# Interleaving independent matmul work into the transform stages of a one-core forward-and-backward kernel, with the TensorE order fixed by hand

## The chip, the cores and the metric

The kernel runs on one core of one Trainium2 chip. The metric is the device time of one execution in microseconds (us). Before the change the median was 1783.06 us in 5 runs (1782.24 to 1788.13).

Engines are named as the profile names them: PE is TensorE with its matmuls, PEld the weight loads of TensorE, DVE is VectorE, ACT is ScalarE, POOL is GpSimd, SP is SyncE. PSUM is the memory that the matmuls of this kernel write to; *evicting* a result means copying it out of PSUM.

## The reference, cut to what matters

The reference is a transformer-like block and its whole backward pass. S is 2048 rows, D is 576 columns, F is 4608 hidden columns, all in bfloat16.

```python
def _A_ref(x, w_r, w_i):                    # spectral filter
    X = rfft2(x.astype(float32)) * (w_r + 1j * w_i)
    return irfft2(X, s=(S, D)).astype(bfloat16)

def _B_ref(x, w_gate, w_up, w_down):        # gated bilinear unit
    return ((x @ w_gate) * (x @ w_up)) @ w_down

def _fwd_reference(x, ..., c, w_mod):
    sa, ca, ga, sb, cb, gb = split6(silu(c) @ w_mod)
    h = layernorm(x) * (1 + ca) + sa
    x = x + ga * _A_ref(h, w_r, w_i)
    h = layernorm(x) * (1 + cb) + sb
    return x + gb * _B_ref(h, w_gate, w_up, w_down)

def reference(..., grad_out):
    out, vjp = jax.vjp(_fwd_reference, ...)   # A_x, A_w_r, A_w_i, B_w_gate, B_w_up, B_w_down, c, w_mod
    return (out, *vjp(grad_out))              # nine outputs
```

## The kernel before

The FFTs are done as matmuls with table matrices. The kernel has three parts.

- **Head.** The six modulation vectors come from blocks of `w_mod`. Then come the layernorm, the forward transform in 8 *fold* steps and 8 *pair* steps, and the inverse transform over 16 row tiles, which yields `h2T`, the input of the gated unit. Beside this runs work that needs none of it: `ghhT = w_down @ (grad_out * gb)^T`. It consists of 72 *ghh units* of 10 matmuls of 512 columns each.
- **Main loop.** 18 iterations over pairs of F-blocks do gate, up, their gradients and the weight gradients.
- **Tail.** This has the layernorm backward with folds, the backward pairs, the backward inverse with the second layernorm backward, the `w_mod` gradients (*finish blocks*) and the down-projection of the forward output (the `po` matmuls).

The framework has a scheduler that chooses each engine's order. `manual_schedule` switches it off for an engine, whose order is then that of the program. Before the change only the main loop had it.

The parts that the change touches, with cuts:

```python
def d_inverse(j, wk, T, ut, fps, ev):          # inverse transform of one row tile
    pv = fps.tile([128, 2, 512], FP32, name="pv", tag="fa")
    ...                                        # 6 matmuls into pv
    vt = wk.tile([128, 2, FQ], BF, name="vt", tag="vt", bufs=3)
    evac(vt[:], pv[:, :, 0:FQ], ev)
    py = fps.tile([128, 2, 512], FP32, name="py", tag="fa")
    ...                                        # 4 matmuls on vt into py
    return py[:, :, 0:288]

with ExitStack() as hs:                        # head
    fps = pool(hs, "fps", bufs=2, space=PSUM)
    gps = pool(hs, "gps", bufs=2, space=PSUM)
    ...
    for hf in range(2):
        t8 = slice(8 * hf, 8 * hf + 8)
        nc.gpsimd.dma_start(gon[:, t8, 0:D], go_v[:, t8, :])
        nc.vector.tensor_tensor(out=gon[:, t8, 0:D], in0=gon[:, t8, 0:D], in1=bc(mods[:, MGB, :], 8), op=MUL)
        nc.vector.tensor_copy(gon[:, t8, D:DP], gon[:, t8, 512:D])
        nc.sync.dma_start_transpose(out=goT[:, t8, :, :]..., in_=gon[:, t8, :]...)
    ...
    for t0 in range(0, NT, 2):
        ...                                    # layernorm, modulation
        fold(wk, h, t0, hT, T, fps, "a" if (t0 // 2) % 2 == 0 else "v")
    for i in range(8):
        ...
        X = pair_fwd(i, wk, gt, T, hT, fps, "aaaa")
        Y = cmul(wk, X, load_wp(wk, i), False)
        pair_inv(i, Y, gbt, ut, fps, "va")
    for t0 in range(0, NT, 2):
        for j in range(2):
            py = d_inverse(t0 + j, wk, T, ut, fps, "a")
            nc.scalar.copy(halves(yg[:, j, :]), py)
        ...                                    # residual, second layernorm -> h2p
        if t0 % 8 == 6:
            nc.sync.dma_start_transpose(out=h2T[:, t8, :, :]..., in_=h2p[:, t8, :]...)

    for fb in range(NFB):                      # 36 blocks, 2 ghh units each
        ...
        for k in range(2):
            pg = gps.tile([128, 2, 512], FP32, name="ghp", tag="gh")
            for b in range(2):
                ts_ = slice(8 * k + 4 * b, 8 * k + 4 * b + 4)
                for m in range(5):
                    r = slice(0, 128) if m < 4 else slice(64, 128)
                    nc.tensor.matmul(pg[:, b, :], lhsT=wdT[r, m, :], rhs=goT[r, ts_, m, :], start=(m == 0), stop=(m == 4))
            nc.scalar.copy(st[:, 8 * k:8 * k + 8, :], pg[:]...)

with ExitStack() as bs:                        # main loop
    ...
    bs.enter_context(tc.manual_schedule(engines={ET.PE}))
    ...

with ExitStack() as ts:                        # tail: the same step functions, then
    ...
    def finish_block(b, q):
        ...
        nc.vector.reciprocal(out=rc[:], in_=(opcb if b in (MSB, MCB) else opca))
    ...
    wdr = [slot(2, [128, 18, D], "wdr0"), up.tile([128, 18, D], BF, name="wdr1")]
    ...                                        # loads of w_down
    for tp_i in range(NT // 2):                # down-projection, 8 pairs of row tiles
        ...                                    # loads of hl, x1, grad_out
        for j in range(2):
            po = ops.tile([128, 2, 512], FP32, name="po")
            for fb in range(NFB):
                for h in range(2):
                    nc.tensor.matmul(po[:, h, 0:288], lhsT=hl[:, fb, j * 128:(j + 1) * 128], rhs=wdr[fb // 18][...], ...)
```

Of the kernel before, what the change touches and what calls it, by code (L numbers as in the profile page):

```python
# [8 lines left out]

FP32 = mybir.dt.float32  # L10
BF = mybir.dt.bfloat16
# [86 lines left out]
def build(ctx, tc, A_x, A_w_r, A_w_i, B_w_gate, B_w_up, B_w_down, c_in, w_mod, grad_out,  # L98
# [23 lines left out]
    gx1_d = dram("gx1_d", [128, NT, D], BF)  # L122
    ghhT_d = dram("ghhT_d", [F, S], BF)
# [11 lines left out]
    nc.vector.memset(ones_bf[:], 1.0)  # L135
    ones_f = glob.tile([128, 128], FP32, name="ones_f")
    nc.vector.memset(ones_f[:], 1.0)
    mods = glob.tile([128, 6, D], BF, name="mods")
# [42 lines left out]
    def fold(wk, h, t0, hT, T, fps, eng):  # L181
# [4 lines left out]
        nc.vector.tensor_tensor(out=eo[:, :, 545:576], in0=h[:, :, 257:288], in1=h[:, :, 319:288:-1], op=SUB)  # L186
        r2 = slice(t0 * 8, t0 * 8 + 16)
# [10 lines left out]
    def pair_fwd(i, wk, gt, T, hT, fps, ev):  # L198
        k2a, k2b = PAIRS[i]
        zt = wk.tile([128, 2, 2, FQ], BF, name="zt", tag="w")  # L200
        for kk, kap in enumerate((k2a, k2b)):
            pz = fps.tile([128, 2, 512], FP32, name="pz", tag="fa")
            for c in range(2):
                for mi in range(3):
                    m = (2 * c, 2 * c + 1, 4)[mi]
                    nc.tensor.matmul(pz[:, c, 0:FQ], lhsT=hT[:, m, kap, :], rhs=T["RD"][:, c, mi, :], start=(mi == 0), stop=(mi == 2))
            evac(zt[:, kk, :, :], pz[:, :, 0:FQ], ev[kk])
        X = wk.tile([128, 2, 2, FQ], BF, name="X", tag="w")
        for kk in range(2):
            px = fps.tile([128, 2, 512], FP32, name="px", tag="fa")  # L210
            C, Sn, nC, nS = (gt[:, kk, v, :] for v in range(4))
            if i == 0:
                terms = [[(C, kk, 0), (Sn, kk, 1)], [(nS, kk, 0), (C, kk, 1)]]
            elif kk == 0:
                terms = [[(C, 0, 0), (Sn, 0, 1), (Sn, 1, 0), (nC, 1, 1)], [(nS, 0, 0), (C, 0, 1), (C, 1, 0), (Sn, 1, 1)]]
            else:
                terms = [[(C, 0, 0), (Sn, 0, 1), (nS, 1, 0), (C, 1, 1)], [(nS, 0, 0), (C, 0, 1), (nC, 1, 0), (nS, 1, 1)]]
            for c in range(2):
                n = len(terms[c])
                for k, (w, kz, cz) in enumerate(terms[c]):  # L220
                    nc.tensor.matmul(px[:, c, 0:FQ], lhsT=w, rhs=zt[:, kz, cz, :], start=(k == 0), stop=(k == n - 1))
            evac(X[:, kk, :, :], px[:, :, 0:FQ], ev[2 + kk])
        return X

    def pair_inv(i, Y, gbt, ut, fps, ev):
        for part in range(2):
            fcs = (0, 1) if part == 0 else (2,)
            pb = fps.tile([128, 2, 2, NT, 2, 8], FP32, name="pb", tag="fa")
            for b, fc in enumerate(fcs):
                fs = slice((0, 128, 161)[fc], (128, 256, 289)[fc])  # L230
                for kind in range(2):
                    if i == 0:
                        terms = [(kind, 0, 1), (kind, 1, 0)]
                    elif kind == 0:
                        terms = [(0, 0, 1), (0, 1, 0), (1, 0, 1), (1, 1, 0)]
                    else:
                        terms = [(0, 0, 2), (0, 1, 1), (1, 0, 0), (1, 1, 3)]
                    n = len(terms)
                    for k, (kk, c, v) in enumerate(terms):
                        nc.tensor.matmul(pb[:, b, :, :, kind, :], lhsT=Y[:, kk, c, fs], rhs=gbt[:, kk, v:v + 2, :], start=(k == 0), stop=(k == n - 1))  # L240
            nb = len(fcs)
            dst = ut[:, fcs[0]:fcs[0] + nb, :, :, i * 16:i * 16 + 16].rearrange("p f c j x -> p f (c j) x")
            evac(dst, pb[:, 0:nb].rearrange("p f c j k q -> p f (c j) (k q)"), ev[part])
# [21 lines left out]
    def d_inverse(j, wk, T, ut, fps, ev):  # L265
        pv = fps.tile([128, 2, 512], FP32, name="pv", tag="fa")
        for c in range(2):
            for fc in range(3):
                nc.tensor.matmul(pv[:, c, 0:FQ], lhsT=ut[:, fc, c, j, :], rhs=T["IR"][:, c, fc, :], start=(fc == 0), stop=(fc == 2))
        vt = wk.tile([128, 2, FQ], BF, name="vt", tag="vt", bufs=3)  # L270
        evac(vt[:], pv[:, :, 0:FQ], ev)
        py = fps.tile([128, 2, 512], FP32, name="py", tag="fa")
        for h in range(2):
            for c in range(2):
                rhs = vt[:, c, 0:288] if h == 0 else vt[:, c, 288:0:-1]
                nc.tensor.matmul(py[:, h, 0:288], lhsT=T["BDI"][:, (1 if h == 1 and c == 1 else 0), :], rhs=rhs, start=(c == 0), stop=(c == 1))
        return py[:, :, 0:288]

    def halves(ap):
        return ap.rearrange("p (h x) -> p h x", h=2)  # L280

    with ExitStack() as hs:
        tp_ = pool(hs, "htab")
        wk = pool(hs, "hwk", bufs=15)
# [7 lines left out]
        with tc.high_priority():  # L292
            c_bf = tp_.tile([128, 5], BF, name="c_bf")
            nc.vector.memset(c_bf[:], 0.0)
            with nc.allow_non_contiguous_dma(reason="tiny c load"):
                nc.sync.dma_start(c_bf[:, 0:4], c_in[0, 0:512].rearrange("(m q) -> q m", q=128))
                nc.sync.dma_start(c_bf[0:64, 4:5], c_in[0, 512:576].rearrange("(m q) -> q m", q=64))
            c_f = tp_.tile([128, 5], FP32, name="c_f")
            nc.vector.tensor_copy(c_f[:], c_bf[:])
            sig = tp_.tile([128, 5], FP32, name="sig")  # L300
            nc.scalar.activation(out=sig[:], in_=c_f[:], func=ACT.Sigmoid)
            nc.vector.tensor_tensor(out=sc_col[:], in0=c_f[:], in1=sig[:], op=MUL)
            tmp5 = tp_.tile([128, 5], FP32, name="tmp5")
            nc.vector.tensor_scalar(out=tmp5[:], in0=sig[:], scalar1=-1.0, scalar2=1.0, op0=MUL, op1=ADD)
            nc.vector.tensor_tensor(out=tmp5[:], in0=tmp5[:], in1=c_f[:], op=MUL)
            nc.vector.tensor_scalar(out=tmp5[:], in0=tmp5[:], scalar1=1.0, scalar2=None, op0=ADD)
            nc.vector.tensor_tensor(out=dsl_col[:], in0=tmp5[:], in1=sig[:], op=MUL)
            sc_bf = tp_.tile([128, 5], BF, name="sc_bf")
            nc.vector.tensor_copy(sc_bf[:], sc_col[:])
            nc.vector.tensor_copy(sc_col[:], sc_bf[:])  # L310
            sc_rep = tp_.tile([128, 5, 128], BF, name="sc_rep")
            nc.vector.tensor_copy(sc_rep[:], sc_bf[:].unsqueeze(2).to_broadcast([128, 5, 128]))

            def mod_block(b, eng):
                wm = u4w.tile([128, 5, D], BF, name="wm", tag="wm", bufs=2)
                eng.dma_start(wm[:, 0:4, :], w_mod[0:512, b * D:(b + 1) * D].rearrange("(m q) n -> q m n", q=128))
                eng.dma_start(wm[0:64, 4, :], w_mod[512:576, b * D:(b + 1) * D])
                ps = gps.tile([128, 2, 512], FP32, name="modps", tag="gh")
                for h in range(2):
                    for m in range(5):  # L320
                        K = KD[m]
                        nc.tensor.matmul(ps[:, h, 0:288], lhsT=sc_rep[0:K, m, :], rhs=wm[0:K, m, h * 288:(h + 1) * 288], start=(m == 0), stop=(m == 4))
                dst = halves(mods[:, b, :])
                if b in (MCA, MCB):
                    nc.vector.tensor_scalar(out=dst, in0=ps[:, :, 0:288], scalar1=1.0, scalar2=None, op0=ADD)
                else:
                    nc.vector.tensor_copy(dst, ps[:, :, 0:288])

            mod_block(MGB, nc.sync)
            gon = slot(2, [128, NT, DP], "gon")  # L330
            goT = u4.tile([128, NT, 5, 128], BF, name="goT")
            for hf in range(2):
                t8 = slice(8 * hf, 8 * hf + 8)
                nc.gpsimd.dma_start(gon[:, t8, 0:D], go_v[:, t8, :])
                nc.vector.tensor_tensor(out=gon[:, t8, 0:D], in0=gon[:, t8, 0:D], in1=bc(mods[:, MGB, :], 8), op=MUL)
                nc.vector.tensor_copy(gon[:, t8, D:DP], gon[:, t8, 512:D])
                nc.sync.dma_start_transpose(out=goT[:, t8, :, :].rearrange("q t m p -> q (t m) p"), in_=gon[:, t8, :].rearrange("p t d -> p (t d)"))
# [431 lines left out]
```

## Time and profile before

| Part, in the profiled run | us | what it does |
|---|---|---|
| head, to the first full gate matmul | 392.5 | folds, pairs, inverse, ghh units |
| main loop, to its last gradient matmul | 992.0 | 18 iterations of mostly 55.75 us |
| tail | 396.0 | backward transforms, down-projection |
| span | 1780.5 | |

The page of the profile before gives the busy time of each engine over the span, then the PE row and its granted clock in 40 equal slices, in tenths. Only these three lines are needed:

```profile
PE 1580.8 (89%) x11196; PEld 1029.6 (58%) x11196; DVE 762.4 (43%) x1743; ACT 515.4 (29%) x881; POOL 203.2 (11%) x365
...
PE   3499999638999999999999999999999789966794
...
PEclk9699999559999999999999999999999989978897
```

PE is the engine that bounds the kernel, and the middle is full. The holes lie at both ends: slices 1, 2, 8 and 9 in the head, and several of the last nine in the tail. In slices 8 and 9 the clock is at half.

The view of stretches before has a line for each stretch. Its columns are: the stretch in us and its length; the busy us and instruction counts of PE, PEld, DVE, ACT and POOL; the granted PE clock; the DMA share; and GB/s.

```profile
40.00:60.00 20.00, 3.37 (x21) 1.92 (x18) 7.96 (x23) 4.61 (x8) 0.65 (x2) 0.50 0.90 142
100.00:150.00 50.00, 50.00 (x212) 16.68 (x210) 1.56 (x2) 20.42 (x21) 0.00 (x0) 1.00 0.44 138
320.00:360.00 40.00, 25.49 (x97) 13.63 (x96) 24.20 (x64) 18.78 (x32) 9.06 (x17) 0.50 0.58 165
360.00:390.00 30.00, 5.90 (x21) 2.80 (x20) 11.96 (x29) 8.12 (x14) 10.05 (x17) 0.50 0.62 127
1411.00:1427.00 16.00, 7.26 (x73) 3.69 (x71) 6.01 (x17) 4.55 (x8) 3.78 (x10) 0.73 1.05 380
1567.00:1634.00 67.00, 44.98 (x241) 22.10 (x240) 63.89 (x153) 32.95 (x47) 14.61 (x27) 0.84 0.50 150
...
1674.00:1755.00 81.00, 73.44 (x583) 56.39 (x583) 9.24 (x13) 5.11 (x8) 6.50 (x12) 1.00 0.45 139
```

At 100 to 150 us PE does ghh units alone and DVE is idle (1.56 of 50 us). At 320 to 390 us the inverse transform runs alone, and PE is both idle and slow. In the tail the inverse is bound by DVE (63.89 of 67 us) while PE works 45 us at a clock of 0.84, and afterwards the down-projection runs alone with every other engine nearly idle. So work that would fill a hole stands beside it, at the wrong time.

The timeline of PE before, within the inverse, shows why that stretch is slow. Its columns are the start, the time, the engine, line and operation, the tiles and shapes, the count, and in brackets the idle time before and what ended it.

```profile
339.31 1.66 PE L269 MATMUL pv<-T_IR,ut 128*128 128x290 bf16 x6
341.75 1.12 PE L276 MATMUL py<-vt,T_BDI 128*128 128x288 bf16 x4 [0.79 <-ACT vt L153]
344.51 1.61 PE L269 MATMUL pv<-T_IR,ut 128*128 128x290 bf16 x6 [1.65 <-ACT yg L378]
```

PE makes `pv`, waits for ACT to copy it out, makes `py`, and waits for ACT again: two round trips for each row tile, with nothing else to do. The view of PE's waits before sums them up (line that waits, what it waited for, us in total, times, the longest):

```profile
PE modps L322 <- DMA wm<-in_w_mod_dram: 26.0, 5, 13.6
PE py L276 <- ACT vt L153: 16.8, 22, 2.1
...
PE abp L473 <- DMA wgu<-in_B_w_gate_dram: 13.5, 1, 13.5
```

Finally, the timeline before where ghh units run alone gives the cost of a unit. ACT evicts one unit in each of these `ghh_st` lines.

```profile
119.89 0.09 PEld L410 LDWEIGHTS <-wdT 64*128 64x128 bf16 x1 [0.42 <-issue]
...
120.21 0.55 PEld L410 LDWEIGHTS <-wdT 128*128 128x128 bf16 x4 [0.23 <-issue]
...
121.60 1.01 ACT L411 CAST ghh_st<-ghp 128x1024 bf16<-128x1024 f32 x1 [1.56 <-PE ghp L410]
...
124.18 1.01 ACT L411 CAST ghh_st<-ghp 128x1024 bf16<-128x1024 f32 x1 [1.56 <-PE ghp L410]
```

A unit takes 124.18 - 121.60 = 2.58 us (2.575 as a mean over two), so the 72 units are 185 us of PE work.

### The profile page before, as it was taken

The page shows a single profiled execution, that of the slowest core. Times are in us where ns is not written, and L with a number is a line of the kernel's source. Part 1 is how long each engine was busy: PE and PEld are TensorE (multiplying, and loading weights), DVE is VectorE, ACT ScalarE, POOL GpSimd, SP SyncE. Part 2 cuts the span into 40 slices and gives each one's busy share as a digit, 9 for nine tenths or more (in the row PEclk, how much of TensorE's full clock was granted, in tenths as well). Part 3 has the DMA queues.
Part 4 walks back from the last instruction along what each step waited for, and adds up shares of the span by engine and source line. Part 5 has one row for each costly group of instructions (what it writes and reads, how often), then busy time and mean ns, then how long its engine had stood idle before and what let it go on. Part 6 is the DMA issues. An engine that isn't in the chain of part 4 may idle for free. (4 is left out here: it accounts for less than half of the span.)

```text
span 1780.5 us, 28313 instructions
## 1 busy us (share of the span) xinstructions
PE 1580.8 (89%) x11196; PEld 1029.6 (58%) x11196; DVE 762.4 (43%) x1743; ACT 515.4 (29%) x881; POOL 203.2 (11%) x365
## 2 busy tenths in 40 slices
PE   3499999638999999999999999999999789966794
PEld 1234444315667766677666776667766657733563
DVE  4601111634423454234542345423454685689211
ACT  2334444521232222312223122231222233244101
POOL 1000010221100111001110011100101121121100
PEclk9699999559999999999999999999999989978897
DMA  9444563577745776467866577645765966544551
GB/s 265 95 140 146 156 148 115 166 147 159 149 105 115 148 146 153 84 125 155 143 134 116 112 158 146 143 96 120 158 130 116 306 223 193 174 137 136 169 169 58
DMA packets 416708, 260.59 MB, mean 146 GB/s; under 512 B 332704, under 2 KB 382112, under 8 KB 416576
## 3 DMA queue, kind: packets, MB, share of 16 engines
q1 hardware_dynamic: 382944, 140.33, 38.3%
q0 software_dynamic: 28448, 99.59, 20.7%
q10 hardware_dynamic: 5184, 18.88, 2.9%
q8 instruction: 87, 1.43, 0.3%
q14 instruction: 45, 0.37, 0.1%
HBM read 103.76 MB, written 76.56 MB: 101 GB/s over the span
## 5 line engine op out<-in xcount | busy, mean ns | idle before, releaser
L502 PE MATMUL abp<-wT,guT 128*128 128x288 bf16 x1152 | 283.0, 286 | 0.0
L501 PE MATMUL abp<-wT,ggT 128*128 128x288 bf16 x1152 | 283.0, 286 | 0.0
L485 DVE TENSOR_TENSOR guT<-ghh,gT 128x512 bf16<-128x512 bf16 x144 | 61.2, 425 | 501.7 <-DMA out_dram<-wl 381.7
L479 PE MATMUL abp<-h2T,wgu 128*128 128x512 bf16 x1152 | 263.7, 382 | 0.0
L507 DVE TENSOR_TENSOR acc<-acc,abp 128x288 f32<-128x288 f32 x544 | 240.8, 453 | 20.4 <-PE abp L502 5.3
L523 PEld LDWEIGHTS <-h2p 128*128 128x128 bf16 x2304 | 225.4, 98 | 27.1 <-issue 0.5
L410 PE MATMUL ghp<-goT,wdT 128*128 128x512 bf16 (+1 forms) x720 | 215.8, 382 | 0.6 <-ACT ghh_st L411 0.6
L479 PEld LDWEIGHTS <-wgu 128*128 128x128 bf16 x1152 | 107.4, 98 | 151.8 <-issue 34.2
L693 PE MATMUL po<-wdr,hl 128*128 128x288 bf16 x1152 | 157.9, 291 | 14.7 <-ACT mo L694 14.4
L515 PE MATMUL gwp<-gon,hh_sf 128*128 128x288 bf16 x1152 | 146.6, 288 | 6.1 <-DMA hh_sf<-hhT 5.5
L516 ACT CAST so<-gwp 128x288 bf16<-128x288 f32 x72 | 28.7, 399 | 397.2 <-PE gwp L515 397.2
L693 PEld LDWEIGHTS <-hl 128*128 128x128 bf16 x1152 | 112.4, 99 | 53.2 <-issue 23.8
L515 PEld LDWEIGHTS <-hh_sf 128*128 128x128 bf16 x1152 | 113.1, 98 | 36.7 <-DMA hh_sf<-hhT 7.6
L501 PEld LDWEIGHTS <-ggT 128*128 128x128 bf16 x1152 | 112.7, 98 | 30.1
L502 PEld LDWEIGHTS <-guT 128*128 128x128 bf16 x1152 | 112.7, 98 | 30.1
L523 PE MATMUL gwp<-gu_sf,h2p 128*128 128x256 bf16 x1152 | 128.7, 273 | 0.4 <-ACT wo L524 0.4
L410 PEld LDWEIGHTS <-wdT 128*128 128x128 bf16 (+1 forms) x720 | 64.1, 97 | 112.1 <-issue 71.4
L523 PE MATMUL gwp<-gg_sf,h2p 128*128 128x256 bf16 x1152 | 128.7, 273 | 0.0
L491 POOL DMA_DIRECT2D hhT_d<-hhT x36 | 33.3, 925 | 804.8 <-DVE hhT L483 758.0
L481 ACT CAST gT<-abp 128x512 bf16<-128x512 f32 x144 | 84.4, 586 | 103.2 <-PE abp L479 103.2
L524 ACT CAST wo<-gwp 128x256 bf16<-128x256 f32 x144 | 53.4, 372 | 192.3 <-PE gwp L523 192.3
L411 ACT CAST ghh_st<-ghp 128x1024 bf16<-128x1024 f32 x72 | 72.9, 1012 | 99.6 <-PE ghp L410 96.0
(169 smaller groups left out, 1576.2 us busy)
## 6 DMA issues: line engine op xcount, KB each, us to landing
ghhT_d<-ghh_st ACTq DMA_DIRECT2D x36, 512.0 KB, 3.3
ghh<-ghhT_d POOLq DMA_DIRECT2D x36, 512.0 KB, 8.5
hhT_d<-hhT POOLq DMA_DIRECT2D x36, 512.0 KB, 6.5
hl<-hhT_d SPq DMA_DIRECT2D x32, 576.0 KB, 4.7
out_dram<-wo SPq DMA_DIRECT2D x36, 256.0 KB, 2.3
out_dram<-so SPq DMA_DIRECT2D x36, 144.0 KB, 1.9
wdr<-in_B_w_down_dram SPq DMA_DIRECT2D x4, 1296.0 KB, 12.0
gbt<-tab_GB POOLq DMA_DIRECT2D x16, 320.0 KB, 4.1
```

The source lines that it names most:

```text
L410: nc.tensor.matmul(pg[:, b, :], lhsT=wdT[r, m, :], rhs=goT[r, ts_, m, :], start=(m == 0), stop=(m == 4))
L411: nc.scalar.copy(st[:, 8 * k:8 * k + 8, :], pg[:].rearrange("f b (t p) -> f (b t) p", p=128))
L479: nc.tensor.matmul(pts[k][i][:], lhsT=wgu[:, 4 * i + m, cs], rhs=h2T[:, ts_, m, :], start=False, stop=(m == 3))
L481: nc.scalar.copy(dst[:], pts[k][i][:])
L485: nc.vector.tensor_tensor(out=guT[:, ts_, :], in0=ghh[:, ts_, :], in1=gu[0][:], op=MUL)
L501: nc.tensor.matmul(pu[:, 0:288], lhsT=ggTs[j][:, t, :], rhs=wT[:, 0, j, hs_], start=(j == 0), stop=False)
L502: nc.tensor.matmul(pu[:, 0:288], lhsT=guTs[j][:, t, :], rhs=wT[:, 1, j, hs_], start=False, stop=(j == G - 1))
L507: nc.vector.tensor_tensor(out=dst, in0=dst, in1=pu[:, 0:288], op=ADD)
L515: nc.tensor.matmul(pw[:, 0:288], lhsT=hh_sf[:, j, t, :], rhs=gon[:, t, h * 288:(h + 1) * 288], start=(t == 0), stop=(t == NT - 1))
L523: nc.tensor.matmul(pw[:], lhsT=h2p[:, t, m * 128:(m + 1) * 128], rhs=sf[:, :, t, :], start=(t == 0), stop=(t == NT - 1))
L524: nc.scalar.copy(wo[:, m, :], pw[:].rearrange("q j f -> q (j f)"))
L693: nc.tensor.matmul(po[:, h, 0:288], lhsT=hl[:, fb, j * 128:(j + 1) * 128], rhs=wdr[fb // 18][:, fb % 18, h * 288:(h + 1) * 288], start=(fb ...
```

## The change

The intent is to let the transforms and the independent matmuls run at the same time on PE. The change has these parts:

1. The step functions are split at the points where PE waits for another engine (`pair_fwd` becomes `pair_z` and `pair_x`, `d_inverse` becomes `d_inv_v` and `d_inv_y`, and so on). The transforms become generators that yield how many units fit at that point, and `interleave` draws the units. Within the transforms the steps are also pipelined by one or two (the next `pv` is made before this `py`).
2. The order of PE is fixed by hand in the head and the tail too.
3. `goT` and `h2T` are made by PE transposes with an ACT eviction, instead of DMA transposes. The factor `gb` goes into goT's eviction as a scale.
4. Four reciprocals leave the tail: two are computed in the head and read back from memory.
5. Loads stand earlier, and the last iteration's weight gradients are kept back as 13 units of filler for the tail.

```diff
+    def interleave(steps, fill):
+        owed = 0.0
+        for n in steps:
+            owed += n
+            while owed >= 1:
+                owed -= 1
+                next(fill, None)
...
     with ExitStack() as hs:
+        hs.enter_context(tc.manual_schedule(engines={ET.PE}))
...
-                nc.sync.dma_start_transpose(out=goT[:, t8, :, :]..., in_=gon[:, t8, :]...)
+            for m in range(5):
+                d0 = (0, 128, 256, 384, 448)[m]
+                ptr = gps.tile([128, 8, 128], BF, name="goTp", tag="gh")
+                for t in range(8):
+                    nc.tensor.transpose(ptr[:, t, :], gon[:, 8 * hf + t, d0:d0 + 128], ident[:])
+                nc.scalar.activation(out=goT[:, t8, m, :], in_=ptr[:], func=ACT.Copy, scale=gbc[:, m:m + 1])
...
+        def head_fft():
+            for t0 in range(0, NT, 2):
...
+                fold_s1(fold_eo(wk, h), t0, hT, T, fps, "a")
+                yield 2
...
+            yield from pairs(wk, gsp, T, hT, ut, fps, False, on_x, lambda i, X: None, 1)
...
+                    if t + 1 < NT:
+                        vt[t + 1] = d_inv_v(t + 1, wk, T, ut, fps, "a")
+                    nc.scalar.copy(halves(yg[:, j, :]), d_inv_y(vt[t], T, fps))
+                    if t >= 4:
+                        h2t_tile(t - 4)
+                    yield 1
...
+        def ghh_units():
...
+                    yield
+        gh = ghh_units()
+        interleave(head_fft(), gh)
+        for _ in gh:
+            pass
...
-        bs.enter_context(tc.manual_schedule(engines={ET.PE}))
+        ts.enter_context(tc.manual_schedule(engines={ET.PE}))
...
-                nc.vector.reciprocal(out=rc[:], in_=(opcb if b in (MSB, MCB) else opca))
+                nc.gpsimd.dma_start(rc[:], rc_d[0 if b in (MSB, MCB) else 1])
...
+        def fill():                              # tail's filler
+            for k, _ in enumerate(last_grads):   # 13 units of the last weight gradients
+                yield
+                if k == 3:
+                    late["wdr"] = [slot(2, [128, 18, D], "wdr0")]
+                    load_wdr(0)
+            ...
+            load_hl(hl, 0)
+            late["wdr"].append(up.tile([128, 18, D], BF, name="wdr1"))
+            load_wdr(1)
+            ...                                  # down-projection, one yield per 18 matmuls
+        fl = fill()
+        interleave(tail_t1(), fl)
+        interleave(tail_rest(), fl)
```

## The prediction

> **What bounds the kernel now.** The tensor engine, but fully only in the middle. From the view of stretches:
> - Main loop (392.5 to 1385 us): 56.3 us per iteration, PE 100% busy at clock 1.00. The change leaves its order alone.
> - Head (0 to 392.5 us): PE is full only from about 100 to 313 us. At 40-60 us it is busy 3.4 of 20 us, at 320-370 us about 60% at clock 0.50, then nearly idle until the first weights land (waits of 13.5 and 9.0 us). The inverse transform runs alone here: the scheduler has used up the independent ghh matmuls.
> - Tail (1385 to 1780.5 us, 395.5 us): PE is low at 1411-1427 (7.3 of 16 us), 1567-1634 (45 of 67 us, DVE 64) and 1634-1674 (22 of 40 us, clock 0.62); then the last down-projection matmuls run alone until 1755, then 25 us without PE.
>
> The Trainium skill ("TensorE: Matmul & The Clock Gate", Part 1) says that an idle window of about 3.4 us halves the PE clock. The trace agrees: 0.50 at 320-390 us, so latency-bound stretches pay twice.
>
> **What the change does.** PE order is fixed by hand in head and tail; transform steps are split and independent matmul units put between them: 72 ghh units over folds, pairs and inverse; in the tail 13 units of the last weight gradients, then down-projection units. It also replaces the DMA transposes of goT and h2T (18.1 us for two, 11.8 us for one in the timeline) by 160 PE transposes, moves reciprocals (3.75 us each, four) out of the tail, and starts loads earlier.
>
> **Head, estimated.** A ghh unit alone repeats every 2.575 us (evictions start at 119.03, 121.60, 124.18), so 72 cost 185 us. Folds, pairs, inverse and mod blocks are about 76 us at full-clock rates of the trace (288 columns: 0.125 us; 256: 0.112), PE transposes about 9 us. First steady work at about 31 us; a few us of transitions. The main loop then starts at about 308 us instead of 392.5, and its cold start (19.9 us for the first stage, later some 16.5) goes: 85-90 us saved. ACT (about 5.4 us per fold step) stays just under PE (5.75 us).
>
> **Tail, estimated.**
> - Layernorm backward plus fold: DVE-bound, 8 steps of 8.5-9.8 us as at 1385-1403: about 78 us (88 now).
> - Pairs with half a unit per step: 6.2 + 4.5 us of PE each, about 88 us (94 now).
> - Inverse with two units (2 x 2.25 us) per row tile: 6.25 us x 16 plus sums, about 104 us.
> - About 11 units left and two finish blocks: 28 us; final chain 22 us.
>
> Sum 320 us, 75 us saved. Nearly all is critical: some 266 us of tail matmuls are the floor.
>
> **Prediction: 1612 us, 1580 to 1650. Faster by over 2%: 0.96; within 2%: 0.03; slower: 0.01.**
>
> **What would show it right.** Main iterations still 56.3 us; first gate matmul near 308 us; no 0.50 clock from about 60 us to the head's end; PE at least 90% busy in head and tail; tail about 320 us with DVE near full only in its first 78 us; the final down-projection stretch shrinking from about 80 to under 30 us. PE instructions up, busy time down, because cold matmuls vanish.
>
> **What would make it wrong.** In-order PE: a unit that waits (activations and down weights of the first down-projection units, loaded only after the last gradients; two PSUM buffers) now stalls the transform behind it. Four load buffers held until late column sums could slow the first tail stage beyond 10 us a step. DMA contention (share 1.05 at 10-30 us) could push the start past 31 us. If none occurs and stages overlap better, 1590.

## The result, and the profile after

The changed kernel took 1641.48 us as a median of 9 runs (1637.51 to 1651.21). The kernel before, run on the same chips, took 1783.28 us (16 runs, 1775.55 to 1797.06). The ratio is 0.9203, with a 95% interval of 0.9179 to 0.9227. Ratios here are the mean time of one kernel's fast runs over that of the other's of the same rounds, so they are not quite the ratios of the medians that are quoted.

The time was taken out of the head and the tail. The columns below are from the profiled runs. The changed kernel was profiled twice; in the first profile one iteration of the main loop took 66.13 us instead of 55.75, after a wait for a load, so the second is the better reference.

| us | head | main loop | tail | span |
|---|---|---|---|---|
| before | 392.5 | 992.0 | 396.0 | 1780.5 |
| after, first profile | 324.5 | 992.5 | 329.4 | 1646.4 |
| after, second profile | 325.1 | 981.0 | 330.0 | 1636.1 |
| predicted | 308 | 984 (the rest of the sum) | 320 | 1612 |

The same three lines of the page, after the change (first profile):

```profile
PE 1549.7 (94%) x11381; PEld 1032.0 (63%) x11381; DVE 759.4 (46%) x1749; ACT 524.3 (32%) x896; POOL 206.2 (13%) x373
...
PE   5899998899999999999998999999999986999893
...
PEclk9999999999999999999998999999999998999997
```

PE has 185 more instructions (160 transposes and 25 small matmuls for goT's scale) and 31 us less busy time; its mean granted clock over the span rose from 0.940 to 0.977. The view of stretches after shows the head's early part, a part of its inverse, then the tail's stages in order:

```profile
40.00:60.00 20.00, 18.16 (x89) 6.85 (x89) 8.49 (x27) 12.48 (x17) 0.78 (x4) 0.91 0.51 141
240.00:260.00 20.00, 17.49 (x101) 8.33 (x99) 16.07 (x42) 12.26 (x20) 5.24 (x10) 1.00 0.75 246
1317.00:1360.00 43.00, 34.25 (x317) 25.90 (x315) 33.84 (x90) 17.45 (x31) 10.43 (x23) 0.95 0.85 277
1360.00:1376.00 16.00, 5.57 (x36) 3.86 (x35) 14.50 (x38) 2.17 (x3) 4.04 (x9) 0.71 1.03 368
1407.00:1489.00 82.00, 81.42 (x672) 65.21 (x673) 61.65 (x85) 28.22 (x46) 15.26 (x33) 1.00 0.68 206
1489.00:1589.00 100.00, 93.87 (x728) 68.80 (x727) 63.49 (x155) 36.80 (x53) 21.12 (x39) 0.97 0.65 205
1589.00:1621.50 32.50, 29.20 (x222) 21.58 (x221) 14.41 (x34) 10.46 (x16) 7.55 (x14) 0.95 0.66 201
```

The head is filled from 40 us on, the backward pairs are full (81.42 of 82 us), and the stretch of down-projection alone shrank from 81 to 32.5 us. One hole is left, at 1360 to 1376 us in the tail, where PE works 5.57 of 16 us and the DMA share is above 1. Within the inverse of the head PE is busy 17.49 of 20 us, not all. The timeline of PE there shows what is left of the two round trips:

```profile
249.08 0.92 PE L322 MATMUL pv<-T_IR,ut 128*128 128x290 bf16 x6
250.78 0.65 PE L332 MATMUL py<-vt,T_BDI 128*128 128x288 bf16 x4 [0.79 <-ACT yg L484]
251.33 0.44 PE L472 MATMUL h2Tp<-ident,h2p 128*128 128x128 bf16 x5
251.61 2.63 PE L525 MATMUL ghp<-goT,wdT 128*128 128x512 bf16 x10
```

A unit of ghh hides one round trip, and `pv` takes 0.92 us at full clock instead of 1.66. One wait stays, that of `py` for a PSUM buffer: it stands behind `pv` with nothing between. The view of PE's waits after names what is left:

```profile
PE s1p L200 <- DVE eo L189: 15.7, 7, 5.4
PE po L843 <- DMA wdr<-in_B_w_down_dram: 11.1, 1, 11.1
PE gbps L418 <- DVE sc_bf L390: 10.0, 1, 10.0
...
PE py L332 <- ACT yg L484: 3.9, 5, 0.8
```

The first of these is the folds waiting for DVE (by stretch, 10.2 us in the head, 5.4 of them before the first fold, and 5.6 in the tail), the second the hole at 1360 us, the third the start.

### The profile page after: what moved, and what is told of

Its sections match the earlier page's. It is cut to its first block, busy times and chain, and to the rows that moved or that the text cites. A ratio compares the mean times of both kernels' runs of the same rounds, so it can differ in the third digit from the quotient of the medians.

```text
span 1646.4 us, 28704 instructions
## 1 busy us (share of the span) xinstructions
PE 1549.7 (94%) x11381; PEld 1032.0 (63%) x11381; DVE 759.4 (46%) x1749; ACT 524.3 (32%) x896; POOL 206.2 (13%) x373
## 5 line engine op out<-in xcount | busy, mean ns | idle before, releaser
L525 PE MATMUL ghp<-goT,wdT 128*128 128x512 bf16 (+1 forms) x720 | 191.6, 386 | 0.0
L843 PE MATMUL po<-wdr,hl 128*128 128x288 bf16 x1152 | 155.5, 295 | 21.3 <-DMA wdr<-in_B_w_down_dram 11.1
L584 PE MATMUL gwp<-gon,hh_sf 128*128 128x288 bf16 x1152 | 150.2, 292 | 7.4 <-DMA hh_sf<-hhT 7.4
```

The source lines that it names most:

```text
L584: nc.tensor.matmul(pw[:, 0:288], lhsT=hh_sf[:, j, t, :], rhs=gon[:, t, h * 288:(h + 1) * 288], start=(t == 0), stop=(t == NT - 1))
```

## The experiments

The leading theory is that the gain is PE time that was idle or half clocked, now filled by independent matmuls. Against it stand three rivals: that the gain comes from the rest of the change (split and pipelined steps, PE transposes, earlier loads, fewer reciprocals); that fixing the order by hand, more than the interleaving, is what brings it; and, for the 29 us missing to the predicted point, that either the transitions stall PE or some work was under-costed. Letters in the texts name such theories: A1 says that the hand order is itself needed for the gain, D that the written interleaving is most of it, E that the other parts are, H what the PE transposes are worth, and I that moving a few whole units by hand mends the stalls.

Twelve kernels were run, one of them the changed kernel itself as a control, in three groups that share runs of the kernel before. Each has 4 runs, one of which is profiled; medians, ranges and ratios are as above. All outputs are right.

### e1: the head written one after the other

```diff
-        interleave(head_fft(), gh)
+        for _ in head_fft():
+            pass
         for _ in gh:
             pass
```

The hand order stays, but all ghh units come after the transform.

> The changed kernel, but in the head all transform steps stand before all 72 ghh units in PE order, nothing between them. Theory A (the head's gain is independent matmuls under the latency of the transform): the first gate matmul moves from 323.5 us to about 410 us (folds 45, pairs 80, inverse 60 us alone, then 72 x 2.575 us), so about 1725 us in all, with the PE clock at 0.50 in long stretches. Rival B (the gain is the missing DMA transposes and the earlier loads, and the interleaving adds little): at most 40 us slower than the changed kernel, below 1680 us.

Measured: 1687.34 us (1686.79 to 1696.91), ratio 0.9472 (0.9434 to 0.9511). The head grew to 376.7 us from 325, and tail and main loop stayed (329.4 and 979.2). Stretches of this kernel, first the folds with the first pairs, then the ghh units:

```profile
33.70:80.00 46.30, 25.73 (x183) 18.88 (x184) 27.90 (x78) 28.78 (x46) 4.88 (x18) 0.63 0.42 116
...
188.00:374.00 186.00, 185.63 (x717) 57.74 (x716) 0.00 (x0) 72.53 (x73) 4.35 (x8) 0.99 0.48 143
```

Without units between them this first stretch runs at a clock of 0.63 with PE busy 25.73 of 46.30 us (the folds alone, 33.7 to 62.8 us, at 0.50), and the units then take 186 us alone with no DVE work at all. That is the cause which the prediction named, and it is worth 52 us in the head. I had expected about 85 us, and the rival at most 40; both missed, and part of the head's gain does not come from interleaving.

### e2: the tail written one after the other

```diff
             load_wdr(1)
+            yield
             wdr = late["wdr"]
...
-        interleave(tail_t1(), fl)
-        interleave(tail_rest(), fl)
+        for _ in range(14):
+            next(fl)
+        for _ in tail_t1():
+            pass
+        for _ in tail_rest():
+            pass
```

The last weight gradients run first, then the transforms, then the down-projection.

> The changed kernel, but in the tail the 13 gradient units come first, then the whole transform, then all down-projection units. Theory A: the transform alone is bound by DVE and latency (about 90 + 70 + 75 us), the down-projection after it takes some 175 us alone, so the tail grows from 329 us to about 430 us, 1740 us in all, slower than the changed kernel by 100 us. Rival B (tail gain from the reciprocals taken out and earlier loads): below 1680 us.

Measured: 1721.71 us (1719.54 to 1723.83), ratio 0.9648 (0.9610 to 0.9686). The tail took 413.6 us against 330.0, so the fill is worth 84 us there. It is even longer than the tail of the kernel before (396.0), whose scheduler could still mix what the program wrote apart: there the first `po` matmul stands at 1426.9 us, among the transforms.

### e3: the same program, with the order of PE left to the scheduler

```diff
-        hs.enter_context(tc.manual_schedule(engines={ET.PE}))
...
-        ts.enter_context(tc.manual_schedule(engines={ET.PE}))
+        bs.enter_context(tc.manual_schedule(engines={ET.PE}))
```

Only the main loop keeps the hand order, as in the kernel before.

> The changed kernel with the program's interleaved order, but the scheduler again orders PE in head and tail (the main loop stays by hand as in both kernels). Theory A1 (the hand-fixed PE order is needed, because the scheduler runs independent units early and leaves the inverse alone): 1660 to 1720 us, with a stretch of low PE at the end of the head. Rival A2 (splitting the steps and writing them interleaved is enough): within 1% of the changed kernel, 1625 to 1655 us.

Measured: 1608.89 us (1608.56 to 1610.98), ratio 0.9022 (0.8994 to 0.9051). The theory that the hand order is needed for the gain falls: giving it up is 30 us *faster*. The head is 306.2 us and the tail 317.9, against 325.1 and 330.0. The timeline of PE of this kernel in the inverse shows what the scheduler does otherwise:

```profile
254.40 0.91 PE L322 MATMUL pv<-T_IR,ut 128*128 128x290 bf16 x6
255.15 0.81 PE L524 MATMUL ghp<-goT,wdT 128*128 128x512 bf16 x3
255.88 0.65 PE L332 MATMUL py<-vt,T_BDI 128*128 128x288 bf16 x4
256.43 0.44 PE L471 MATMUL h2Tp<-ident,h2p 128*128 128x128 bf16 x5
256.80 1.67 PE L524 MATMUL ghp<-goT,wdT 64*128 64x512 bf16 x6
```

It cuts the units: some of a unit's ten matmuls go between `pv` and `py`, the rest behind the transposes. No idle time is left, as its stretch says:

```profile
240.00:260.00 20.00, 19.98 (x125) 10.37 (x124) 16.45 (x40) 14.56 (x23) 5.95 (x11) 1.00 0.64 218
```

PE is busy 19.98 of 20 us where the hand order gave 17.49. Both kernels put about the same number of units into the stages of the head (folds, pairs, inverse, end: 16, 34, 15 and 7 by hand; 14.9, 32.7, 15.1 and 6.9 by the scheduler), apart from the start: the scheduler puts 2.4 units ahead of the first fold and starts the units at 30.4 us instead of 34.6. The wait of `s1p` for `eo` (15.7 us after the change) is gone from the waits of this kernel. The orders of ACT and DVE changed little with it: of their 221 and 297 instructions in the head, 203 and 288 stand in the same order as in the control (e8's group), so nearly all of the difference is PE's order.

### e10: the scheduler's order, with the program written one after the other

This has the edits of e3, e1 and e2 together.

> The scheduler orders PE (as in the run of the scheduler that took 1608.89 us), and the program is written serially: head transform, then ghh units; in the tail gradients, transform, down-projection. Everything else of the change (split steps, PE transposes, reciprocals taken out, earlier loads) stays. Theory D (the interleaved order of the program is what lets the scheduler, or the hand, keep independent units for the late, latency-bound steps): 1700 to 1760 us, with the inverse again alone at a clock of 0.50 in the head. Rival E (the scheduler finds the overlap by itself; splitting, transposes and loads are the gain): within 2% of 1609, below 1640 us.

Measured: 1680.90 us (1678.46 to 1687.43), ratio 0.9416 (0.9382 to 0.9450), with head 336.2, main loop 989.2 and tail 359.9. Both expectations missed; the truth lies between. From the kernel before to this one the gain is some 104 us (medians), and it comes from the parts other than interleaving and hand order. From this one to e3, where the units are written between the steps, it is 72 us more: 30 in the head and 42 in the tail. So the interleaving is about two fifths of what e3 gains. With the other parts of the change in place the scheduler fills many gaps itself: in the inverse (150 to 210 us) PE is busy 59.90 of 60 us at full clock, so theory D's picture was wrong there. It does not find all of them (210 to 334 us: 108.47 of 124), and what order the program has still counts.

### e7: goT and h2T by DMA transposes again

```diff
-                for t in range(8):
-                    nc.tensor.transpose(ptr[:, t, :], gon[:, 8 * hf + t, d0:d0 + 128], ident[:])
-                nc.scalar.activation(out=goT[:, t8, m, :], in_=ptr[:], func=ACT.Copy, scale=gbc[:, m:m + 1])
+            nc.vector.tensor_tensor(out=gon[:, t8, 0:D], in0=gon[:, t8, 0:D], in1=bc(mods[:, MGB, :], 8), op=MUL)
+            nc.vector.tensor_copy(gon[:, t8, D:DP], gon[:, t8, 512:D])
+            nc.sync.dma_start_transpose(out=goT[:, t8, :, :]..., in_=gon[:, t8, :]...)
...                                            # and h2T likewise, every 8 row tiles
```

> The changed kernel with both sets of PE transposes put back to DMA transposes (goT at the start, h2T in two halves), PE order still by hand and interleaved. Theory H (the transposes on PE matter at the start, since the first ghh unit stands behind the first fold in PE's order and goT by DMA lands at 50 to 75 us as in the kernel before, and at the end, where the last h2T by DMA took 21.7 us to land): 25 to 50 us slower, 1665 to 1690 us. Rival (they only move work; what counts is the order): within 10 us of the changed kernel.

Measured: 1660.89 us (1651.44 to 1664.20), ratio 0.9290 (0.9251 to 0.9329). That is some 20 us slower than the changed kernel; the expected 25 to 50 was a little too high. The wait of PE that replaces the transposes:

```profile
PE ghp L519 <- DMA goT<-gon: 13.3, 1, 13.3
```

The first ghh unit starts at 48.2 us instead of 34.6, and the head is 336.5 us, 11 more than the changed kernel's. The first iteration of the main loop took 65.8 us instead of 57.8; the second half of `h2T` landed 21.8 us after its issue, but the profile puts PE's waits there down to loads of gate and up weights (5.7 and 3.7 us), so what h2T's transposes alone are worth is not shown. In the changed kernel the transposes on PE cost little: 7.2 us busy for goT's 80 and 6.7 us for h2T's 80, by their groups.

### e4: all contractions of a ghh unit over 128 rows

```diff
         nc.vector.tensor_copy(gbc[:], gbc_bf[:])
+        nc.vector.memset(gbc[0:64, 4:5], 0.0)
...
-                            r = slice(0, 128) if m < 4 else slice(64, 128)
-                            nc.tensor.matmul(pg[:, b, :], lhsT=wdT[r, m, :], rhs=goT[r, ts_, m, :], ...)
+                            nc.tensor.matmul(pg[:, b, :], lhsT=wdT[:, m, :], rhs=goT[:, ts_, m, :], ...)
```

D is 576, so the fifth block holds only 64 new rows; its other 64 rows repeat the fourth block. Zeros in the scale of the repeated rows let the matmul take all 128 rows.

> The changed kernel, but the fifth contraction piece of a ghh unit (64 rows) is made a full 128-row matmul by zeroing its other 64 rows of goT. Theory C (a 64-row matmul among 128-row ones costs about 0.2 us of exposed weight load[...], twice per group of five: 2.575 us per unit against 10 x 0.216): 72 x 0.42 us = 30 us less PE time in the head, of which 20 to 30 us show: 1612 to 1622 us, ghh evictions alone about 2.16 us apart. Rival: the pitch has another cause (eviction or transposes of the weights), and the time stays within 5 us of the changed kernel.

Measured: 1617.99 us (1612.28 to 1631.01), ratio 0.9081 (0.9031 to 0.9131). The timeline of PE of this kernel, one unit among the pairs:

```profile
160.98 2.32 PE L525 MATMUL ghp<-goT,wdT 128*128 128x512 bf16 x10
163.14 1.04 PE L248 MATMUL pb<-gbt,cA 128*128 128x256 bf16 x8
```

The next work starts 163.14 - 160.98 = 2.16 us later, where a unit took 2.575 us before. PE's busy time fell from 1546.0 us (second profile of the changed kernel) to 1514.0, that is by 32 us; 72 units of 0.42 us are 30. The head went from 325.1 to 300.6 us. So a matmul of fewer rows among full ones cost some 0.2 us each, twice in a unit (the expectation's "per group of five" is a slip: its sum counts two for a unit of ten), and the share of busy time did not show it before.

The Trainium skill ("TensorE: Matmul & The Clock Gate", section "LDWEIGHTS (loading the stationary operand)") says that a load's time depends on the columns and not on the rows. The load itself agrees: 92 ns on average for 64 rows and 98 for 128 rows in the kernel before. The single records of its trace show where the cost is. Full matmuls start 0.216 us apart; the one of 64 rows starts 0.312 us after the full one before it, and the next full one 0.319 us after that, together 0.2 us more. Between full ones a load starts with the matmul before its own (at 119.366 and 119.364 us, for instance), so it is hidden; the load of 64 rows starts only at 119.887, 5 ns before its own matmul. Why it comes so late no run here explains.

The main loop of both kernels has the same odd block and treats it otherwise: its 64-row matmuls for gate and up use different halves of the rows and stand in groups of four, and the two of a pair start 4 ns apart in the traces. For the ghh units such pairing was not tried.

The same page's section "Back-to-back issue gap" gives N / 2.4 + 2.5 ns for a lone matmul of N columns, which is 216 ns at 512. The unit of ten in 2.16 us agrees.

### e5: another order of the loads in the tail's hole

```diff
-            load_hl(hl, 0)
-            late["wdr"].append(up.tile([128, 18, D], BF, name="wdr1"))
-            load_wdr(1)
+            late["wdr"].append(up.tile([128, 18, D], BF, name="wdr1"))
+            for kind, fb0 in (("h", 0), ("h", 9), ("w", 18), ("h", 18), ("w", 27), ("h", 27)):
+                ...                              # hl or w_down, 9 blocks each
```

> The changed kernel with the first half of the second down-weight block issued before the third piece of the activations, so that it does not queue behind a store that waits for DVE. Theory F (the 11.1 us wait of PE for these weights is on the critical path of the first tail stage, because PE is in order): the wait shrinks below 4 us and the kernel gains 5 to 11 us: 1631 to 1637 us. Rival (DVE bounds that stage, so the wait is slack): within 3 us of the changed kernel.

Measured: 1645.13 us (1633.83 to 1654.41), ratio 0.9207 (0.9147 to 0.9267): no gain. PE's wait changed its name, and little of it went away. In this kernel it reads:

```profile
PE po L846 <- DMA hl<-hhT_d: 11.3, 2, 6.9
```

The two loads together held PE up 14.3 us in the changed kernel (11.1 for the weights, 3.2 for `hl`), 13.5 in its second profile and 11.3 here. Together with the DMA share of 1.03 at 368 GB/s in the hole after the change, this points to the amount of bytes that must come in there, not to their order. But the rival, that DVE bounds the stage, fits the time as well: DVE is busy 14.50 of 16 us in the hole. Neither holds the stage at its length alone: in e3, with the same bytes and the same DVE work, it took 83 us (1291.3 to 1374.4) instead of 90. Fewer bytes, or an earlier place for them, was not tried.

### e6: the reciprocals put back into the tail

```diff
-                nc.gpsimd.dma_start(rc[:], rc_d[0 if b in (MSB, MCB) else 1])
+                nc.vector.reciprocal(out=rc[:], in_=(opcb if b in (MSB, MCB) else opca))
```

> The changed kernel with the four reciprocals of 3.75 us put back on DVE in the tail (the stored copies are not read). Theory G (after interleaving the tail is bound by PE, DVE has room): up to 5 us slower, 1640 to 1647 us. Rival (DVE is still on the critical path in the inverse stage): the full 15 us, 1655 us or more.

Measured: 1637.45 us (1637.10 to 1640.49), ratio 0.9171 (0.9144 to 0.9197), so the same time. The tail was 329.4 us against 330.0. First the stretch of the backward inverse in this kernel, then that of the changed kernel (second profile):

```profile
1474.00:1574.00 100.00, 93.02 (x726) 68.17 (x724) 69.77 (x157) 36.68 (x53) 20.02 (x37) 0.98 0.63 199
```

```profile
1478.00:1578.00 100.00, 93.34 (x735) 68.90 (x734) 63.92 (x156) 36.80 (x53) 21.05 (x39) 0.98 0.65 206
```

DVE carries 6 us more in this stretch and PE is as busy as before. DVE has room there, so taking the reciprocals out bought nothing once PE was filled.

### after_again: the changed kernel once more, as a control

> The changed kernel itself, as a control on the chip of the runs sent with it: ratio 0.920 to before, 1637 to 1648 us.

Measured: 1638.63 us (1637.97 to 1649.25), ratio 0.9206 (0.9162 to 0.9250), beside e8, e11 and e12 on one chip. Its profile is the second one quoted above.

### e8: the hand order mended at unit size

```diff
+        for _ in range(2):
+            next(gh)
         interleave(head_fft(), gh)
...
+                    yield 1
                     if t >= 4:
                         h2t_tile(t - 4)
-                    yield 1
```

Two units go ahead of the first fold, as the scheduler does, and the unit in the inverse stands between `py` and the transposes.

> The changed kernel, PE order by hand, with two edits of the order in the head alone: two ghh units before the first fold, and in the inverse the unit between the second product and the transposes of h2T instead of after them. Theory I (the hand order loses to the scheduler because PE, in order, stands at waits that a unit could have covered: 15.7 us at the folds, about 0.5 us per tile in the inverse): the head shortens by 8 to 15 us, the first gate matmul comes at 309 to 315 us, and the kernel takes 1626 to 1634 us. Rival J (what the scheduler gained came from other engines' order or from the tail): within 4 us of the changed kernel.

Measured: 1639.84 us (1635.61 to 1641.91), ratio 0.9190 (0.9160 to 0.9219): no difference from the control. The head's end came 7 us earlier (318.0), but the first stage of the main loop then took longer (from 316.6 to 339.9 us, that is 23.3 us, where the changed kernel's second profile has 18.7, from 324.1 to 342.8), so 2.9 of the 7 us were left, and a stray third iteration of 59.9 us took these. Two of this kernel's waits:

```profile
PE s1p L200 <- DVE eo L189: 11.8, 7, 3.0
...
PE py L332 <- ACT h2T L473: 5.0, 9, 0.6
```

The wait of the folds shrank by only 4 us (the theory had put all 15.7 us at the head's folds, where only 10.2 are) and a new wait came, because `py` now needs the PSUM buffer that the transposes hold. Moving whole units did not reach e3's time: theory I missed, and the time is within rival J's 4 us. Of J's two reasons, the order of other engines hardly differs (see e3), and the tail holds 12 of e3's some 30 us. Whether placing parts of units by hand would reach e3 is open, as that was not tried.

### e12 and e11: the two gains together

e12 has the edits of e3 and e4. e11 has those of e12 and e5.

> The scheduler's PE order together with full 128-row contractions in the ghh units. If the two gains (32 and 23 us) are of different causes, stalls and PE work, they add: 1580 to 1592 us. If the head is then bound by ACT and DVE: 1595 to 1605 us.

> The same with the down-weight halves issued between the pieces of the activations. With the hand order that only moved the wait from the weights to the activations; if the tail's first stage is bound by the bytes that must land, it again gives nothing: within 4 us of the run without it. Otherwise 5 to 10 us faster.

Measured: e12 took 1592.85 us (1590.50 to 1596.55), ratio 0.8931 (0.8902 to 0.8960). It is the fastest kernel and beats both given ones: 46 us under the control on the same chip. Its profile has head 286.6, main loop 980.8, tail 323.1. e3's gain of 30 us and e4's of some 20 nearly add up; the time lies just outside the range of 1580 to 1592 that was expected for a plain sum. e11 took 1595.64 us (1594.51 to 1604.04), ratio 0.8955 (0.8921 to 0.8989), so the order of loads was no help here either.

## Why the prediction was right, and where its size was off

The time, 1641.48 us, lies within 1580 to 1650, 29 us above the point of 1612. Against the second profile (1636.1 us), the head took 17 us more than predicted, the tail 10 more and the main loop 3 less, together 24 us. The other 5 us are the distance of that profile from the median of the nine runs: 1.9 of them are device time outside the profiled span (1637.97 against 1636.1 us), and longer stray iterations of the main loop, as in the first profile, would make up the rest, but that was not tested.

- **"Latency-bound stretches pay twice."** Shown. Before, the inverse ran at 0.50 from 320 to 390 us; after, `pv` takes 0.92 us instead of 1.66, and the clock was full from 58.5 us to 321.3, 3 us before the head's end. In e1, where units are taken out again, the stretch of the folds and first pairs falls to 0.63. The Trainium skill ("TensorE: Matmul & The Clock Gate", Part 1) says that PE's clock halves after an idle window. This trace agrees only in part: before, the clock fell at 319.2 us though no idle time of PE in the 9 us before was longer than 1.4 us (in the last 3.41 us it was busy 1.29), and it stayed at half up to 366 us with waits of at most 1.66 us. So PE need not stand still through such a window to lose its clock.
- **The gain comes from interleaving PE work.** Right in kind, and overstated. Under the hand order the interleaving is worth 52 us in the head (e1) and 84 in the tail (e2). Left to the scheduler, it is worth 72 us (e10 to e3), and some 104 us come from the rest of the change. The PE transposes are some 20 us under the hand order (e7), the reciprocals nothing (e6). How the rest divides among pipelined steps, earlier loads and held-back gradients was not separated.
- **The sums of work.** The sums for head and tail, 308 and 320 us, are close to what the program reaches when PE stalls less: e3, the same program in the scheduler's order, has 306.2 and 317.9, and 1608.89 us in all. The agreement of the totals does not prove each term.
- **The mis-sized step is "a few us of transitions".** In the fixed order these stalls are some 30 us: 19 in the head and 12 in the tail (e3 against the control, 306.2 to 325.1 and 317.9 to 330.0). The stretches confirm that it is waiting: in the head from 30 us on, PE is idle 20.8 us in the control and 6.4 in e3, with 4.4 us less busy time; in the tail, idle 53.3 and 41.6. In the head the folds took 55 us (33.6 to 88.2) instead of 46 (8 steps of 5.75), of which PE waited 4.8 for DVE's `eo`, while matmuls at half clock (up to 38.0 us, and 55.1 to 58.5) make most of the rest. By a reckoning at the same rates made afterwards, the inverse took 72 instead of 66, and from its end to the first gate matmul it was 24.5 instead of 18 (7 units); e3 does not shorten this last part (25.7). I had costed ACT against PE for a fold step and left out that an in-order PE meets DVE's `eo` at the wrong moment. The prediction named the reverse as a risk ("In-order PE: a unit that waits" stalls the transform), with no time for it in the sum; here a transform step waited and held up the units behind it.
- **The first tail stage.** 78 us were predicted and 90 measured (1317 to 1407 us). The hole of 16 us at 1360 holds the wait of 11.1 us for down weights, which the prediction also named as a risk. DVE is busy 33.84 of 43 us in the part before it, 14.50 of 16 in the hole and 13.72 of 31 in the part after it, so "near full" was right only for the hole. The other stages were close: pairs 82 us (88 predicted), inverse 100 (104), rest 32.5 (28), final chain 25 (22).
- **The start, 31 us.** The first fold came at 33.6, after waits of PE of 10.0 us for the vector `sc_bf` and 5.4 us for the first `eo`.
- **Main iterations of 56.3 us.** 55.75 us in nearly all iterations of every profile; before, the mean is 56.5 with the first one (67.3 us) in it, so the 56.3 seems to be an average over longer ones too.
- **PE at least 90% busy in head and tail.** True of most stretches (18.16 of 20, 81.42 of 82, 93.87 of 100 us), false in the inverse of the head (17.49 of 20), in the tail's first stage around the hole, and just missed in the stretch after the tail's inverse (29.20 of 32.5).
- **The last stretch of down-projection under 30 us.** 32.5 us, a near miss. PE's instructions went up and its busy time down, as said.

The prediction had also taken the 2.575 us of a ghh unit as its floor, since PE was 100% busy there. e4 shows that it was not: 16% of it were gaps inside "busy". The Trainium skill ("Perfetto Trace Analysis", section "Identifying the Most-Contended Engine") warns that a matmul's busy share is a poor measure of the distance to the peak and that the share of weight loads is a better one. The trace agrees as to the busy share: 50.00 of 50 us of matmul at 100 to 150 us, where e4 then found 16% to save; weight loads show 16.68 of 50 there.

## What to carry to other kernels

Where one stage is bound by latency and another by matmuls alone, split the first at its waits and write the second's independent work between the parts; the Trainium skill ("Perfetto Trace Analysis", section "Optimization Strategy") suggests interleaving such regimes, and here the whole change took 8%. Having written the program so, try it with the scheduler's order as well as with a fixed one: a fixed order can stall at any step whose input is late (here `s1p`, 15.7 us in all), and here the scheduler, which could cut units into single matmuls, was 30 us better. Before taking a unit's time as its floor because PE shows 100%, divide it by its matmuls and columns, and look for an odd shape among them.

## What the Trainium skill lacked or had wrong

- "TensorE: Matmul & The Clock Gate" says of the weight load that its time does not depend on the rows, which this trace nearly confirms (92 ns for 64 rows, 98 for 128). Neither it nor "TensorEngine Tiling (Array Packing)", which says without a figure that a change of tiling mode drains TensorE, tells what a matmul of 64 rows costs among matmuls of 128: here each adds about 0.2 us, half before and half after it; ten matmuls of 512 columns took 2.575 us with two such among them and 2.16 us without.
- The same page gives two figures for 512 columns, 216 ns for a lone matmul and about 131 ns sustained. This case's stream of full matmuls, with a load before each, ran at 2.16 us for ten, thus at the first, and no two full matmuls of 512 columns in the four traces looked at record by record (before, control, e3, e4) started less than 215 ns apart.
- Part 1 of the same page gives no share of work below which a window counts as idle: here 1.29 us of work in the 3.41 us up to 319.2 us, in short pieces, were too little to keep the full clock.
- No page says how much a hand-fixed order of PE can lose against a scheduler's on the same program: 1638.63 us against 1608.89 here.
